# Gated attention and MoE layer: W2 loaded in four parts, its sums on VectorE, one product beside each up group

## The chip, the cores and the metric

The kernel runs on one core of a Trainium2 chip. The metric is the device time of one execution in microseconds (us); the table below gives the median of seven runs of the kernel before. The engines are called TensorE (PE in the profile; PEld is its weight load), VectorE (DVE), ScalarE (ACT), GpSimd (POOL) and SyncE (SP). Each engine works through its own instructions in the order in which the program puts them; an instruction that waits holds up everything behind it on the same engine.

## The reference

For each of 8 batches with 3008 rows, attention without softmax is multiplied by a gate and sent through a two-layer network:

```
scores = (1/S) * z @ z.T                  # z: 3008 x 64
out    = relu(scores)**2 @ v              # v: 3008 x 256
x      = u * out                          # 3008 x 256
h      = x @ w_in                         # w_in: 256 x 2048
g      = h * sigmoid(1.702 * h)
result = g @ w_out                        # w_out: 2048 x 256
```

The inputs and the result are float32. The kernel works in float16 with float32 accumulation.

## The kernel before, in words

**Tiles.** Rows of a batch are cut into 24 row tiles of 128 (the last one half full) and into 6 chunks of up to 512 (`NJ`, `NCH`). `W1` (w_in) and `W2` (w_out) stay in the on-chip memory as float16. `W2` has 16 slices of 128 rows (`NFF`), and 256 columns.

**Order by hand.** The order of instructions on every engine is the order in which the Python code issues them. Nothing reorders them later; only the waits are added, from what reads and writes what. Each kind of tile has a fixed number of buffers; a new tile takes the buffer of the oldest one and waits until that is no longer read.

**One batch.** Three stages follow each other.

- *Attention.* `attend` (line 270) gives for each chunk a list of steps, each of one or two matmuls; the loop at line 604 walks through them. Between steps the tables `SCHED0` (batch 0) and `SCHED` (later batches) say when `take` issues scores for later chunks, `TURN0` and `LOAD0` when a part of u is transposed on VectorE (`turn_u`) and the next loaded (`load_u`). When a chunk is done, VectorE multiplies it by u (`gate`, line 314), which makes the tile `xt`. In chunks of 47 steps that use half the rows of the array, step 24 on TensorE waits for a signal that passes through POOL's queue after step 23 (`post`, line 82).
- *Up groups and products.* An up group (`up_group`, line 335) makes 2 of 16 slices of the hidden layer for one chunk: 4 matmuls into the bank `hg` (2 buffers), the gelu on ScalarE from `hg` to `gf` (2 buffers), and a scaling on VectorE from `gf` to `gt`. There are 8 groups per chunk (`NFG`), 48 per batch. The first `LAGY` of them, 19, are spread over the steps of the last attention chunk, chunk 5 (line 614); they are called head groups. The other 29 follow in the loop at line 637.
  The second layer of chunks 0 to 3 is done with seven products of half size in place of eight (P1 to P7, lines 401 to 444). They need sums of parts of `gt` (`left_sum`, two instructions each of S1 to S4, on VectorE, one behind each up group from group 8 on) and sums of parts of W2 (`weight_sums`, line 368, into `WT`, once per run). A product is 16 matmuls of 128 columns. P6, P7 and P4 add into the bank that P1 opened, P3 into that of P5, P2 has its own; ScalarE copies the bank of P1 after P1, P6 and P7 (tiles `uP1`, `uP6`, `uP7`), before the next one may add to it. VectorE puts copy and bank together at P2, P7 and P3. In the loop at line 637 one product follows each up group as long as more than two are left: beside groups 19 to 44. Groups 45 and 46 have none, P4 of chunk 3 stands behind group 47, and P3 of chunk 3 behind that.
- *The last two chunks.* Their second layer (`down64`, line 487) is done directly and interleaved with the first scores of the next batch.

**Loading W2.** After attention chunk 4 of batch 0 POOL copies one element of its `xt` (so that it waits for the chunk), issues one 1 MB load of W2 that converts to float16, waits for it, and makes the four sums. Behind these in POOL's queue stand the loads of u and z of batch 1, the copies of z, and the conversion of v.

Of the kernel before, what the change touches and what calls it, by code (L numbers as in the profile page):

```python
# [10 lines left out]
F16 = mybir.dt.float16  # L11
P = 128
# [3 lines left out]
def kernel(  # L16
# [14 lines left out]
    ALU = mybir.AluOpType  # L31
# [5 lines left out]
    NJ = (S + P - 1) // P  # L37
# [39 lines left out]
    ZT, V16, UQ, UT, XT, unit, TT = {}, {}, {}, {}, {}, {}, {}  # L77
# [47 lines left out]
    def first_zt(g):  # L125
        z2 = ZT["st"][g // CB][:, g % CB * CB:(g % CB + 1) * CB]
        zp = ps1.tile([P, CB, P], F16, name="zp", tag="ps1")
        for k in range(CB):
            pe.transpose(zp[:, k, :], z2[:, k, :, :], ident)
        zt = ZT[0][:, g * CB:(g + 1) * CB, :].rearrange("d n p -> d (n p)")  # L130
        nb = CB if g < NCH - 1 else CB - 1
        dst = zt[:, :nb * P].rearrange("d (p n) -> d n p", n=nb)
        if g == 0:
            act.activation(dst, zp[:, :nb, :], AF.Copy, scale=1.0)
        else:
            dve.tensor_copy(dst, zp[:, :nb, :])
        if nb < CB:
            dve.tensor_copy(zt[:, nb * P:], zp[:, nb, :])
# [49 lines left out]

    def turn_u(b, i):
        n = width(i)  # L190
        ut = pu.tile([P, NCC, CH // QW, QW], F32, name="ut", tag="ut")
        UT[b, i] = ut
        dve.transpose(ut[:, :, :n // QW, :].rearrange("p k q t -> p q k t"), UQ.pop((b, i))[:, :n // QW])  # L193
# [171 lines left out]
    LO, HI = slice(0, NFF // 2), slice(NFF // 2, NFF)  # L365
    C0, C1 = slice(0, P), slice(P, D)

    def weight_sums():
        b11, b12, b21, b22 = W2[:, LO, C0], W2[:, LO, C1], W2[:, HI, C0], W2[:, HI, C1]
        t1, t2, t3, t4n = (WT[:, m] for m in range(4))  # L370
        pool.tensor_tensor(t1, b12, b11, ALU.subtract)
        pool.tensor_tensor(t2, b22, t1, ALU.subtract)
        pool.tensor_tensor(t3, b22, b12, ALU.subtract)
        pool.tensor_tensor(t4n, b21, t2, ALU.subtract)

    def left(b, k, h, odd):
        g = GT[b, k, h].rearrange("p f (m o t) -> p f m o t", o=2, t=P)
# [23 lines left out]
    def products():  # L401

        lst = []
        for k in range(NST):
            one = [(k, "P5"), (k, "P6"), (k, "P2"), (k, "P7")]
            lst += [(k, "P1")] + ([(k - 1, "P4"), (k - 1, "P3")] if k else []) + one
        return lst + [(NST - 1, "P4"), (NST - 1, "P3")]

# [110 lines left out]

        return turns, [lambda n=n: step(n) for n in range(len(order))]  # L520

    LAGY = 2 * NFG + 3
    HEAD = 2

    def pieces(b, i):
# [29 lines left out]
    TURN0 = {(i, (38, 28)[i] if i < 2 else NJ + 4 if i < NCH - 1 else 12): i for i in range(NCH)}  # L555
    LOAD0 = {(i, n): i + 2 for i, n in TURN0 if i + 2 < NCH}
    TURN = {(1, NJ + 4): 2, (2, NJ + 4): 3, (4, NJ + 4): 4, (5, 8): 5}
    LOAD = {(3, NJ + 4): 4, (4, NJ + 5): 5}

    FIRST_ZT = {3: 3, 11: 4, 19: NCH - 1}  # L560
# [11 lines left out]
    def take(b, n):  # L572
        if n:
            group = [queue.pop(0) for _ in range(n)]
            scores(b, group)
# [23 lines left out]
    for b in range(B):  # L599
        nup = NCH * NFG  # L600
        sched, turn, load = (SCHED, TURN, LOAD) if b else (SCHED0, TURN0, LOAD0)
        head = 0
        for i in range(NCH):
            for n, step in enumerate(attend(b, i, b == 0 and i < 2)):
                if b == 0 and i == 0 and n == 5:
                    load_u(0, 0)
                if b == 0 and i == 0 and n in FIRST_ZT:
                    first_zt(FIRST_ZT[n])
                if (i, n) in turn:
                    turn_u(b, turn[i, n])  # L610
                if (i, n) in load:
                    load_u(b, load[i, n])
                take(b, sched[i].get(n, 0))
                if i == NCH - 1 and n >= HEAD and (n - HEAD) * LAGY // (2 * NJ - 2 - HEAD) >= head and head < LAGY:
                    up_group(b, head)
                    head += 1
                step()
            if b == 0 and i in (0, 1, NCH - 2):
                hold = const.tile([P, 1], F16, name=f"hold{i}")
                pool.tensor_copy(hold, XT[b, i][:, 0, :1])  # L620
                if i < 2:
                    w1v = moe_w_in.rearrange("(q k c) f -> q c k f", k=NCC, c=QW)
                    for k in range(2 * i, 2 * i + 2):
                        pool.dma_start(W1[k * QW:(k + 1) * QW], w1v[k])
                elif i == NCH - 2:
                    pool.dma_start(W2, moe_w_out.rearrange("(fo p) c -> p fo c", p=P))
                    weight_sums()
        more = b + 1 < B
        if more:
            for i in range(2):  # L630
                load_u(b + 1, i)
            load_z(b + 1)
            for n0 in range(0, NJ, VB):
                load_v(b + 1, n0, sp)
            fill(b + 1)
        downs, prods = down_list(b), products()
        for q in range(head, nup):
            if more and q in (head + 14, head + 20):
                k = int(q == head + 20)
                turn_u(b + 1, k)  # L640
                load_u(b + 1, k + 2)
            up_group(b, q)
            if len(prods) > 2 or q == nup - 1:
                product(b, *prods.pop(0))
        while prods:
            product(b, *prods.pop(0))
        if more:
            while downs[0][0] < NCH - 2:
                down(b, *downs.pop(0))
            for k in range(NCH - 2, NCH):  # L650
                turns, steps = down64(b, k)
                at = {n: 3 - len(turns) for n in turns} | TAIL[len(turns)]
                for n, step in enumerate(steps):
                    take(b + 1, at.get(n, 0))
                    step()
        else:
            for d in downs:
                down(b, *d)
# [30 lines left out]
```

## Time and profile before

| what | value |
|---|---|
| median of seven runs | 1228.67 us (1219.86 to 1232.71) |
| the profiled execution's own time | 1219.86 us |
| its span, first to last instruction | 1217.8 us |
| mean granted clock of TensorE | 0.995 of full speed |
| busy: PE, DVE, ACT, POOL | 1198.5, 825.3, 768.3, 300.5 us |
| W2 load (line 626): start, issue, landing | 81.92, 1.16, 9.0 us after its start |
| four sums of W2 on POOL (lines 371 to 374) | 2.12, 2.45, 2.57, 2.57 us |
| `s` sums of 128x1024 on VectorE (lines 395, 397, 399), mean | 0.84, 0.74, 0.75 us |

The span is that of one execution seen by the hardware profiler; the device time lies about 2 us above it. Durations of matmuls overlap, since the next one starts while the last one drains: four matmuls of 512 columns show 1.03 us, but the next work starts 0.86 us after them. So stages are compared by start times. An idle time in brackets at the end of a timeline row is that of the engine just before the row, with what ended it.

### The profile page before, as it was taken

Reading aid. Unit: us, or ns where it says so; the run is one execution under the profiler, and the core shown is the slowest. Engines: PE = TensorE matmul, PEld = TensorE weight load, DVE = VectorE, ACT = ScalarE, POOL = GpSimd, SP = SyncE. Lnnn points to the kernel's source line nnn. Section 1 sums busy time; section 2 is a strip of 40 time slices with the busy share of each in tenths; the row PEclk is TensorE's granted clock in tenths of the full one; section 3 lists DMA queues with packets and bytes.
Section 4 is the critical chain, followed back from the end, with each engine's and each line's share of the span. In section 5 each row is a group of like instructions: output and inputs, shape, how many; then the busy total and the mean of one; then the engine's idle time right before and its main releaser. Section 6 shows DMA issues by size and latency. Waiting matters only on the chain.

```text
span 1217.8 us, 28022 instructions
## 1 busy us (share of the span) xinstructions
PE 1198.5 (98%) x11691; PEld 713.9 (59%) x11691; DVE 825.3 (68%) x1253; ACT 768.3 (63%) x897; POOL 300.5 (25%) x350
## 2 busy tenths in 40 slices
PE   8999999999999999999999999999999999999998
PEld 3344775567644676446765467544775447755576
DVE  7669956498554985459754597637966479554882
ACT  6776675476854768457683576836667376772763
POOL 5217500353004510045200451005500134001000
PEclk8999999999999999999999999999999999999999
DMA  9953579563794629956299553974449754596012
GB/s 225 170 79 62 171 160 172 97 127 107 145 166 97 143 84 172 149 91 148 88 167 159 85 136 93 188 137 76 143 108 185 133 88 147 114 173 112 1 36 70
DMA packets 370767, 152.31 MB, mean 125 GB/s; under 512 B 313200, under 2 KB 364272, under 8 KB 370640
## 3 DMA queue, kind: packets, MB, share of 16 engines
q1 hardware_dynamic: 328960, 113.16, 48.7%
q0 software_dynamic: 33552, 29.37, 12.8%
q10 hardware_dynamic: 8128, 8.00, 2.2%
q8 instruction: 91, 1.49, 0.5%
q14 instruction: 36, 0.29, 0.1%
HBM read 60.29 MB, written 24.64 MB: 70 GB/s over the span
## 4 chain that ended last, share of the span: by engine, by line
PE 92%; ACT 3%; DMA 2%; DVE 2%; issue 1%; ACTq 0%; SPq 0%
PE o L301 37%; PE hg L342 26%; PE st L424 16%; PE yp L503 6%; PE sc L216 5%; DMA tt<-a 2%; ACT rl L228 1%; PE yp L458 1%; ACT gf L350 1%; DVE gt L351 1%; ACT y L516 1%; DMA zf<-in_z_dram 0%; DVE a L242 0%; DVE zst L123 0%; ACTq L476 0%
## 5 line engine op out<-in xcount | busy, mean ns | idle before, releaser
L350 ACT ACTIVATE gf<-hg 128x1024 f32<-128x1024 f32 (+1 forms) x384 | 386.0, 1007 | 200.4 <-PE hg L342 163.2
L228 ACT ACTIVATE rl<-sc 128x1024 f16<-128x1024 f32 x311 | 307.0, 1024 | 216.1 <-PE sc L216 203.7
L301 PEld LDWEIGHTS <-V 64*128 64x128 f16 (+1 forms) x4052 | 231.9, 94 | 255.1 <-issue 10.5
L342 PE MATMUL hg<-xt,W 128*128 128x512 f16 (+1 forms) x1408 | 354.8, 375 | 4.0 <-ACT gf L350 4.0
L351 DVE TENSOR_SCALAR gt<-gf 128x1024 f16<-128x1024 f32 (+1 forms) x384 | 280.3, 730 | 90.6 <-ACT gf L350 86.2
L301 PE MATMUL o<-a,V 64*128 64x512 f16 (+2 forms) x2010 | 316.5, 373 | 0.4 <-DVE a L242 0.4
L242 DVE TENSOR_TENSOR a<-rl 128x1024 f16<-128x1024 f16 x276 | 192.1, 698 | 181.8 <-ACT rl L228 180.7
L186 POOL DMA_DIRECT2D uq<-in_u_dram x188 | 132.5, 712 | 604.8 <-PE sc L216 444.4
L301 PE MATMUL o<-tt,V 64*128 64x512 f16 (+1 forms) x1762 | 215.1, 376 | 3.8 <-DMA tt<-a 3.8
L342 PEld LDWEIGHTS <-W 128*128 128x128 f16 x1536 | 141.6, 98 | 126.5 <-issue 9.5
L424 PEld LDWEIGHTS <-gt 128*128 128x128 f16 x2048 | 125.1, 98 | 28.9
L216 PE MATMUL sc<-ZT 64*128 64x512 f16 (+1 forms) x692 | 121.7, 367 | 2.6 <-ACT rl L228 1.9
L171 POOL CAST V<-vst 128x512 f16<-128x512 f32 x96 | 90.2, 979 | 61.3 <-DMA vst<-in_v_dram 48.6
L424 PEld LDWEIGHTS <-s 128*128 128x128 f16 x1536 | 93.5, 98 | 19.5
L503 PE MATMUL yp<-W,gt 64*128 64x256 f16 x1664 | 103.9, 269 | 0.0
L503 PEld LDWEIGHTS <-gt 64*128 64x128 f16 x1664 | 80.4, 94 | 19.2 <-POOLq L84 4.0
L318 DVE TENSOR_TENSOR xt<-o,ut 128x512 f16<-128x512 f32 x80 | 51.5, 685 | 38.1 <-PE o L301 38.1
L424 PE MATMUL st<-WT,s 128*128 128x128 f16 x1024 | 67.6, 219 | 0.0
L424 PE MATMUL st<-W,gt 128*128 128x128 f16 x1024 | 67.6, 219 | 0.0
L424 PE MATMUL st<-WT,gt 128*128 128x128 f16 x1024 | 67.6, 219 | 0.0
L216 PEld LDWEIGHTS <-ZT 64*128 64x128 f16 x692 | 38.0, 94 | 41.6 <-issue 9.9
L193 DVE STREAM_TRANSPOSE ut<-uq 128x1024 f32<-128x1024 f32 (+1 forms) x48 | 58.3, 1215 | 0.0
(48 smaller groups left out, 611.2 us busy)
## 6 DMA issues: line engine op xcount, KB each, us to landing
vst<-in_v_dram SPq DMA_DIRECT2D x39, 512.0 KB, 5.0
uq<-in_u_dram POOLq DMA_DIRECT2D x156, 128.0 KB, 3.4
out_dram<-y SPq DMA_DIRECT2D x32, 512.0 KB, 3.7
out_dram<-y ACTq DMA_DIRECT2D x8, 512.0 KB, 4.3
tt<-a SPq DMA_TRANSPOSE x230, 3.6
uq<-in_u_dram POOLq DMA_DIRECT2D x32, 112.0 KB, 3.0
vst<-in_v_dram SPq DMA_DIRECT2D x8, 384.0 KB, 4.6
out_dram<-y ACTq DMA_DIRECT2D x7, 384.0 KB, 5.0
```

The source lines that it names most:

```text
L171: pool.tensor_copy(V16[b][:, n0:n0 + VB, k, :].rearrange("p n (q c) -> p n q c", c=QW), vst.rearrange("p n (q k c) -> p n q k c", k=NCC, c ...
L186: eng.dma_start(uq[k * QW:(k + 1) * QW, :n // QW].rearrange("t q k c -> t q (k c)"), src[:, :, cs])
L193: dve.transpose(ut[:, :, :n // QW, :].rearrange("p k q t -> p q k t"), UQ.pop((b, i))[:, :n // QW])
L216: pe.matmul(sc[:, r, :m * P], zt[h, 2 * kp + r, :], zt[h, (qi + 1) * CB - m:(qi + 1) * CB, :], start=True, stop=True,)
L228: act.activation(rl, sc, AF.Relu, scale=csc)
L242: dve.tensor_tensor(a, rl, rl, ALU.mult)
L301: ins = pe.matmul(acc[c][:, :n], V16[b][h, j, c, :], weights(b, i, j)[h], start=(k, m) == first[c], stop=(k, m) == final[c],)
L342: pe.matmul(hg[:, e, :n], W1[:, c, ff * P:(ff + 1) * P], XT[b, i][:, c, :n], start=(c == 0), stop=(c == NCC - 1),)
L350: act.activation(gf[:, :, :n], hg[:, :, :n], AF.Gelu_apprx_sigmoid, scale=1.0 / FSC)
L351: dve.tensor_scalar(g, gf[:, :, :n], FSC, None, ALU.mult)
L424: pe.matmul(bank[:, m, :], lhs()[:, f, m, :], right[:, ff, :], start=name in ("P1", "P2", "P5") and m == 0 and ff == 0, stop=ff == NFF // ...
L503: ins = pe.matmul(yp[s // per][:, s % per, :], GT[b, k, ff // CB][h, ff % CB, s * P:(s + 1) * P], W2[h, ff, :], start=new, stop=n == last[ ...
```

## The change

- W2 is loaded in four parts of four slices (256 KB each), at steps 4, 10, 27 and 33 of attention chunk 4 of batch 0. Before each, POOL copies one element of the `xt` of chunk 3. Parts 0 and 1 hold the upper half of W2, 2 and 3 the lower.
- The four sums of W2 are issued on VectorE, behind the first, third, fifth and seventh up group of chunk 5 of batch 0.
- `LAGY` is 20 rather than 19: 20 head groups in chunk 5, 28 groups in the loop behind it, in every batch.
- One product is issued behind each of these 28 groups, none after them.
- Within a block the order is P1, (P4 and P3 of the block before), P6, P5, P7, P2. It was P1, (P4, P3), P5, P6, P2, P7.

```diff
+    def load_w2(k):
+        hold = const.tile([P, 1], F16, name=f"hold2{k}")
+        pool.tensor_copy(hold, XT[0, NCH - 3][:, 0, :1])
+        fs = slice(k * CB, (k + 1) * CB)
+        pool.dma_start(W2[:, fs], moe_w_out.rearrange("(fo p) c -> p fo c", p=P)[:, fs])
+
     def weight_sums():
...
-        pool.tensor_tensor(t1, b12, b11, ALU.subtract)
-        pool.tensor_tensor(t2, b22, t1, ALU.subtract)
-        pool.tensor_tensor(t3, b22, b12, ALU.subtract)
-        pool.tensor_tensor(t4n, b21, t2, ALU.subtract)
+        return [
+            lambda: dve.tensor_tensor(t1, b12, b11, ALU.subtract),
+            lambda: dve.tensor_tensor(t2, b22, t1, ALU.subtract),
+            lambda: dve.tensor_tensor(t3, b22, b12, ALU.subtract),
+            lambda: dve.tensor_tensor(t4n, b21, t2, ALU.subtract),
+        ]
...
-            one = [(k, "P5"), (k, "P6"), (k, "P2"), (k, "P7")]
+            one = [(k, "P6"), (k, "P5"), (k, "P7"), (k, "P2")]
...
-    LAGY = 2 * NFG + 3
+    LAGY = 2 * NFG + 4
...
+    LOADW = {4: 0, 10: 1, NJ + 3: 2, NJ + 9: 3}
...
+                if b == 0 and i == NCH - 2 and n in LOADW:
+                    load_w2(LOADW[n])
...
                     up_group(b, head)
                     head += 1
+                    if b == 0 and head in (1, 3, 5, 7):
+                        weight_sums()[head // 2]()
...
-                elif i == NCH - 2:
-                    pool.dma_start(W2, moe_w_out.rearrange("(fo p) c -> p fo c", p=P))
-                    weight_sums()
...
             up_group(b, q)
-            if len(prods) > 2 or q == nup - 1:
-                product(b, *prods.pop(0))
-        while prods:
             product(b, *prods.pop(0))
```

More of the change, by code (lines that the diff above doesn't have):

```diff
@@ L616 @@
                     head += 1
+                    if b == 0 and head in (1, 3, 5, 7):
+                        weight_sums()[head // 2]()
                 step()
-            if b == 0 and i in (0, 1, NCH - 2):
+            if b == 0 and i < 2:
                 hold = const.tile([P, 1], F16, name=f"hold{i}")
                 pool.tensor_copy(hold, XT[b, i][:, 0, :1])
[L621 to L624, printed above, removed]
-                elif i == NCH - 2:
-                    pool.dma_start(W2, moe_w_out.rearrange("(fo p) c -> p fo c", p=P))
-                    weight_sums()
+                w1v = moe_w_in.rearrange("(q k c) f -> q c k f", k=NCC, c=QW)
+                for k in range(2 * i, 2 * i + 2):
+                    pool.dma_start(W1[k * QW:(k + 1) * QW], w1v[k])
         more = b + 1 < B
```

## The prediction

> **What bounds the kernel now.** First the page's busy shares and its wait list. TensorE is busy for 98% of the span, and all its waits for a compute engine or a DMA come to 14 us, so only two things can shorten the kernel: less matmul work (the change has the same 11,691 matmuls), or fewer of those holes. VectorE and ScalarE have a third of the span free as a mean, which says nothing of single stages.
>
> ```profile
> PE 1198.5 (98%) x11691; PEld 713.9 (59%) x11691; DVE 825.3 (68%) x1253; ACT 768.3 (63%) x897; POOL 300.5 (25%) x350
> ...
> PE hg L342 <- ACT gf L350: 5.0, 13, 1.1
> PE o L301 <- DMA tt<-a: 3.8, 3, 2.6
> PE sc L216 <- ACT rl L228: 1.9, 2, 1.0
> ```
>
> The largest entry, 5.0 us in 13 waits of an up group's matmuls for the gelu on ScalarE, is the one the change touches. TensorE's timeline puts five of the 13 (3.0 us) in chunk 5 of batch 0, and one of 0.25 us at the end of each of the 8 batches. So next the timelines of POOL, DVE and PE around 91 to 106 us (start, duration, instruction, idle time before it):
>
> ```profile
> 91.02 2.12 POOL L371 TENSOR_TENSOR WT<-W 128x1024 f16<-128x1024 f16 x1 [7.93 <-DMA W<-in_moe_w_out_dram]
> 93.22 2.44 POOL L372 TENSOR_TENSOR WT<-W,WT 128x1024 f16<-128x1024 f16 x1
> 95.63 2.57 POOL L373 TENSOR_TENSOR WT<-W 128x1024 f16<-128x1024 f16 x1
> 98.16 2.57 POOL L374 TENSOR_TENSOR WT<-W,WT 128x1024 f16<-128x1024 f16 x1
> ...
> 89.92 0.69 DVE L351 TENSOR_SCALAR gt<-gf 128x1024 f16<-128x1024 f32 x1 [0.38 <-ACT gf L350]
> 91.16 7.58 DVE L351 TENSOR_SCALAR gt<-gf 128x1024 f16<-128x1024 f32 x3 [0.55 <-ACT gf L350]
> 98.67 2.61 DVE L395 TENSOR_TENSOR s<-gt 128x1024 f16<-128x1024 f16 x1
> 101.19 0.68 DVE L351 TENSOR_SCALAR gt<-gf 128x1024 f16<-128x1024 f32 x1
> ...
> 94.86 1.02 PE L342 MATMUL hg<-xt,W 128*128 128x512 f16 x4 [0.31 <-ACT gf L350]
> 97.39 1.02 PE L342 MATMUL hg<-xt,W 128*128 128x512 f16 x4 [1.13 <-ACT gf L350]
> 99.91 1.84 PE L342 MATMUL hg<-xt,W 128*128 128x512 f16 x4 [1.13 <-ACT gf L350]
> ...
> 91.00:106.10 15.10, 12.12 (x50) 4.90 (x49) 14.94 (x14) 7.30 (x8) 15.00 (x10) 0.89 0.13 40
> ```
>
> While POOL makes the four sums, each gt instruction of VectorE takes 2.5 us in place of 0.69, exactly the length of one POOL sum; ScalarE then has no free gf buffer, and TensorE no free hg bank. The last row is the stage table (busy us by engine, then granted clock 0.89): inside it, from 100 to 103.4 us, the clock was granted at half, which doubles the matmuls there (1.84 us for four in place of 1.03).
>
> **The change, part by part.**
>
> 1. *The sums leave POOL.* What that stretch costs is read from starts, since matmul durations overlap. In batch 0 chunk 5 runs from its first up group at 81.21 us to the first product at 112.29: 31.08 us. In batch 1 the same work, with no hole, runs from 232.90 to 258.68: 25.78 us. The difference is 5.3 us: 3.0 of shown idle time, half of 3.4 us at half clock (1.7), and about 0.6 of pipeline refills. It is all on TensorE's path. All of it goes if nothing else stalls there: -5.3 us.
>
> Here two pages stand behind the rows. The Trainium skill's "SBUF — State Buffer" (SBUF: two separate sides) says that VectorE and GpSimd share a port pair that one holds for a whole instruction while the other blocks. The rows agree for these sums, but not in general: at 254.77 a POOL copy took 5.97 us beside VectorE instructions that stayed at 0.68, so the later one can also give way. "TensorE: Matmul & The Clock Gate" (Part 1: The HAM clock gate) says that an idle window of about 3.4 us halves the clock. Here 3 us of scattered idle time was followed by the half clock, 3.4 us long. By the page's rule these holes are too short, and the clock's 1.7 us would stay for some other reason: a gain of 3.6. I go by the row, 5.3, because no other stretch after the start has the half clock.
>
> 2. *The sums on VectorE.* Four more instructions of 128x1024 f16. The nearest row is s<-gt: 0.68 us, 0.60 from start to start: 2.4 us in all. They stand behind the 1st, 3rd, 5th and 7th up group, where VectorE idles 0.4 to 0.7 us before each gt. The tight place is the third sum: the transpose of u (1.1 us) follows it at once, so gt, sum and transpose take 0.6 + 0.6 + 1.1 = 2.3 us in a group of 1.28, and the next gt is 1.0 us late. How much is free: in the trace the gt at 91.16 (the first of three in 7.58 us) ended 1.8 us late and TensorE was 0.47 late (94.86, where the pace gives 94.39), so about 1.4 us is absorbed. 1.0 fits. Bounds: 0 and 0.6 us; I take 0.2.
>
> 3. *W2 in four parts, in chunk 4.* POOL's queue gets four copies of 0.2 us and four issues. The W1 parts of the same 256 KB took 0.55 us each to issue and 6.9 to 11.2 to land; the single W2 load 1.16 and 9.0. POOL is free at 69.86 (the u load ends). Parts 0 and 1 are issued by 71.4. Next in that queue is the signal (line 84) that step 24 of chunk 4 on TensorE waits for; step 23 ends near 74.7, so 3.3 us are spare. A rule speaks against it: in the same section of "SBUF — State Buffer" the Trainium skill says that VectorE can keep GpSimd from writing descriptors, a 620 ns transfer becoming 3100. With 3.1 per issue the two parts would end near 76.5, and TensorE would stand 1.8 us. In this trace 188 u issues from POOL took 0.63 to 1.2 us, many beside busy VectorE; I take the row: nothing. Parts 2 and 3 follow the signal: issued by 76.3, landed by 83 to 87.5. The first sum needs parts 0 and 1 (landed by 82.6) near 84.1, the second needs the rest near 86.7. A wait of up to 0.8 us there is below the 1.4 absorbed: nothing. Behind W2, POOL's loads for batch 1 start some 20 us earlier; the second half of u still waits for VectorE's transpose in chunk 5. SP's transposes and V loads follow the z copies, and the V casts, which stretch VectorE's instructions to 1.09, fall a few products after chunk 5, as they do in batch 1 (from 266.9) without a TensorE wait.
>
> 4. *One product beside each up group.* Before, up groups 45, 46 and 47 stand without a product between them, and gelu is slower than an up group. TensorE and ScalarE at the end of batch 1:
>
> ```profile
> 303.49 1.89 PE L342 MATMUL hg<-xo,W 128*128 128x512 f16 x8
> 305.63 1.02 PE L342 MATMUL hg<-xo,W 128*128 128x512 f16 x4 [0.25 <-ACT gf L350]
> ...
> 304.55 1.94 ACT L350 ACTIVATE gf<-hg 128x1024 f32<-128x1024 f32 x2 [0.46 <-PE hg L342]
> ```
>
> Two groups of 0.864 us from 303.49 end at 305.22; the third starts at 305.63, 0.41 us late. In even batches (384 columns, 0.65 us a group) it is 157.33 and 157.75: 0.42. With a product of 0.89 us after every group ScalarE has 1.5 to 1.75 us per gelu of 0.8 to 1.0. Eight batches: -3.3 us. The products and up groups themselves only move.
>
> 5. *A 20th head group.* It moves 0.864 us of matmul from the next stage into chunk 5, and the groups there stand 1.28 us apart on TensorE (0.864 and 2.2 attention steps of 0.189) in place of 1.30. VectorE needs 1.20 for gt and sum, and two xt gates of 0.6. In batch 1 it worked without a pause from 248.6 to 262.4 and was 0.3 us behind gelu near the end. The tighter pace adds 0.02 per group over 12 groups: 0.55 behind, still within 1.4. I take nothing; bound 0.3 us a batch, 2.4.
>
> 6. *P6 straight after P1.* In block 0 only one up group now lies between P1 and P6, which adds into the same bank and waits for ScalarE's copy uP1. Rows: gelu at 112.49, uP at 113.41 for 0.38, so done at 113.79; the product after the next up group starts at 114.05. 0.26 us to spare, with semaphores to be paid out of it. Later blocks have P4 and P3 between. Bounds: 0 and 0.5 us a batch; I take 0.07, 0.6 in all. P7 and P2 in the new order have two groups or more of cover, and P4's copy now precedes the next stage by one group more.
>
> *Sum*: -5.3 - 3.3 + 0.2 + 0.6 = -7.8 us on the profiled execution's 1219.86 (span 1217.8 and 2 us around it): 1212.1. That execution was the fastest of the seven; the median is 8.8 us above, for reasons no row shows, so I take the same 7.8 off it: **1220.9**, 0.63% less.
>
> **The rivals.**
>
> *The small waits give half of it back.* Parts 5 and 6 at their upper bounds: 2.4 + 4.0 in place of 0.6, so 1220.9 + 5.8 = 1226.7, no measurable change. For it: VectorE without pause in chunk 5, and 0.26 us of slack. Against: no TensorE wait there in seven batches.
>
> *The stall only changes its cause.* If the last W2 parts land late, the second sum waits at the head of VectorE's queue, gt behind it, gelu behind that, TensorE last. Landing at 92 rather than 87.5 would cost about 92 - 86.7 - 1.4 = 3.9 us and perhaps the clock's 1.7 again: the 5.3 is gone, 1226.5. Against: transposes, which slowed W1, are over by chunk 4 (DMA share 0.12 from 67 to 81 us).
>
> *More than the trace shows.* The slow half of the seven runs may hold a longer stall here: some 5 us more, 1216. Nothing speaks for it but the spread.
>
> *Slower.* P6 waits for uP1 in every batch, and each wait sends the clock to half for 3.4 us (1.7 lost): with a 0.6 us wait, 8 x 2.3 = 18 us, 1239. It decides from 1.75 us a batch (14 us). Against: the 0.25 us holes at each batch's end were never followed by a half clock.
>
> **How the numbers follow.** A measurement of this kernel can tell about 0.5%, 6.1 us, so faster means below 1222.5. The forecast has 0.60 with an own range of 1217 to 1224, five sixths of it below the limit; the half given back 0.19; the stall with another cause 0.06; more gain 0.09; slower 0.06. Faster 0.50 + 0.09 = 0.59; same 0.10 + 0.25 = 0.35; slower 0.06. The range takes in the gain of 1216 with its own spread and both cases near 1226.5: 1213 to 1229.
>
> **What would show it.** Right: gt at 0.7 us through chunk 5 of batch 0, the chunk near 26.6 us from first up group to first product, no half clock after the start, POOL without sums, no wait of hg before group 47, the wait of hg for gelu down from 5.0 to below 1 us. Wrong: a gt or WT instruction waiting for the W2 DMA, a wait of st for uP in each batch, a wait at step 24 of chunk 4, or a half clock at some other place.

## The result, and the profile after

| | before | after |
|---|---|---|
| device time, median | 1225.96 us (64 executions, 1215.24 to 1244.56) | 1214.41 us (27 executions, 1207.67 to 1236.13) |
| ratio, 95% interval | | 0.9915, 0.9897 to 0.9933 |
| profiled execution, its span | 1219.86 us, 1217.8 us | 1210.50 us, 1208.5 us |
| mean granted clock | 0.995 | 0.996 |

The kernel became faster by 0.85%, some 10 us; 7.8 us (0.63%) were forecast. The ratio leaves out slow executions, those more than 1.5% above the fastest of their kernel, so it is not the quotient of the two medians (0.9906, 11.6 us). A second series of the changed kernel, 22 executions beside other executions of the one before, gave 1219.26 us and 0.9941 (0.9919 to 0.9963), some 7 us. So the size is known to a few microseconds only, and the experiments below are largely about the reason for that.

First the busy shares of the kernel after, from its profile (busy time, share of the span, instructions):

```profile
PE 1194.9 (99%) x11691; PEld 723.2 (60%) x11691; DVE 822.7 (68%) x1257; ACT 769.7 (64%) x897; POOL 314.9 (26%) x352
```

Then its list of TensorE's waits (who waits, for whom: total us, times, longest):

```profile
PE o L301 <- DMA tt<-a: 2.5, 2, 2.1
PE sc L216 <- ACT rl L228: 1.9, 2, 1.0
...
PE hg L342 <- ACT gf L350: 0.5, 1, 0.5
```

The up groups' wait for gelu has gone from 13 times and 5.0 us to once and 0.5. VectorE has four instructions more, the sums of W2. The wait for transposed tiles fell from 3.8 to 2.5 us, which no part of the forecast had. Now the timelines of POOL and VectorE where the moved work stands:

```profile
70.32 0.77 POOL L372 DMA_DIRECT2D W<-in_moe_w_out_dram  x1
71.40 0.75 POOL L372 DMA_DIRECT2D W<-in_moe_w_out_dram  x1
...
75.43 0.74 POOL L372 DMA_DIRECT2D W<-in_moe_w_out_dram  x1 [0.26 <-issue]
76.79 0.74 POOL L372 DMA_DIRECT2D W<-in_moe_w_out_dram  x1
...
83.97 0.68 DVE L378 TENSOR_TENSOR WT<-W 128x1024 f16<-128x1024 f16 x1
84.72 0.69 DVE L351 TENSOR_SCALAR gt<-gf 128x1024 f16<-128x1024 f32 x1
86.03 0.69 DVE L351 TENSOR_SCALAR gt<-gf 128x1024 f16<-128x1024 f32 x1 [0.62 <-ACT gf L350]
86.64 0.69 DVE L379 TENSOR_TENSOR WT<-W,WT 128x1024 f16<-128x1024 f16 x1
...
89.05 0.69 DVE L380 TENSOR_TENSOR WT<-W 128x1024 f16<-128x1024 f16 x1
89.65 1.10 DVE L193 STREAM_TRANSPOSE ut<-uq 128x896 f32<-128x896 f32 x1
90.68 1.25 DVE L351 TENSOR_SCALAR gt<-gf 128x1024 f16<-128x1024 f32 x2
91.85 0.69 DVE L381 TENSOR_TENSOR WT<-W,WT 128x1024 f16<-128x1024 f16 x1
```

The parts of W2 landed 4.6 us (median) after their issue and no sum waits for one. The sums take 0.69 us, and gt beside them too, 2.5 before. The tight place (third sum, transpose of u, two gt) passes without an idle TensorE. Next, the stretches that set the end, on TensorE: first and last up group of chunk 5 of batch 0 with the first product, the one hole between them, and the products of batch 1, first and last, with the first `down64` matmul behind them:

```profile
81.16 1.03 PE L342 MATMUL hg<-xt,W 128*128 128x512 f16 x4
...
102.48 1.02 PE L342 MATMUL hg<-xt,W 128*128 128x512 f16 x4 [0.53 <-ACT gf L350]
...
107.63 1.03 PE L342 MATMUL hg<-xt,W 128*128 128x512 f16 x4
108.49 1.06 PE L432 MATMUL st<-W,gt 128*128 128x128 f16 x16
...
254.44 1.06 PE L432 MATMUL st<-W,gt 128*128 128x128 f16 x16
...
299.25 1.03 PE L342 MATMUL hg<-xo,W 128*128 128x512 f16 x4
300.11 1.06 PE L432 MATMUL st<-WT,gt 128*128 128x128 f16 x16
301.00 1.03 PE L342 MATMUL hg<-xo,W 128*128 128x512 f16 x4
301.87 1.06 PE L432 MATMUL st<-W,s 128*128 128x128 f16 x16
302.86 0.50 PE L511 MATMUL yp<-W,gt 64*128 64x256 f16 x6
```

The starts that they are compared with, in the kernel before: chunk 5 and first product of batch 0, the same of batch 1, and the first `down64` matmul of batch 1.

```profile
81.21 1.03 PE L342 MATMUL hg<-xt,W 128*128 128x512 f16 x4
...
112.29 1.06 PE L424 MATMUL st<-W,gt 128*128 128x128 f16 x16
...
232.90 1.03 PE L342 MATMUL hg<-xt,W 128*128 128x512 f16 x4
...
258.68 1.06 PE L424 MATMUL st<-W,gt 128*128 128x128 f16 x16
...
308.37 0.50 PE L503 MATMUL yp<-W,gt 64*128 64x256 f16 x6
```

Chunk 5 of batch 0 is 108.49 - 81.16 = 27.33 us from first up group to first product; before it was 31.08 with one group of 0.864 less. So 31.08 + 0.86 - 27.33 = 4.6 us went there. The later batches need 26.64 (25.78 before), so 0.69 us of stall is left. The up groups of the batch end follow a product without idle time: from first product to first `down64` matmul a batch takes 46.71 or 48.42 us where it took 47.98 or 49.69. That is 1.27 less, of which 0.86 is the group that moved to chunk 5, so 0.41 per batch and 3.3 us in all. The spans differ by 9.4: 4.6 + 3.3, and 1.4 in attention and down of batches 1 to 7 (515.5 us before, 514.1 after). There the waits for transposed tiles that the list shows fell from 1.2 to 0.5 us. But this stretch isn't steady: two more profiles of the kernel before, without any edit, have 517.1 and 516.4 us, and one more of the changed kernel 515.1.

The stretch that the forecast showed at a mean clock of 0.89 now reads as follows (length, then busy PE, PEld, DVE, ACT, POOL, granted clock, DMA share, GB/s):

```profile
91.00:106.10 15.10, 14.57 (x72) 6.83 (x70) 14.85 (x24) 11.35 (x12) 8.00 (x10) 1.00 0.69 88
```

TensorE is busy for 14.57 of 15.10 us at full clock, against 12.12 at 0.89. The DMA share rose from 0.13 to 0.69: batch 1's loads, no longer queued behind the sums on POOL, have moved into chunk 5.

### The profile page after: what moved, and what is told of

It reads as the page before. It is cut to its first block, busy times and chain, and to the rows that moved or that the text cites. A ratio compares the mean times of both kernels' runs of the same rounds, so it can differ in the third digit from the quotient of the medians.

```text
span 1208.5 us, 28037 instructions
## 1 busy us (share of the span) xinstructions
PE 1194.9 (99%) x11691; PEld 723.2 (60%) x11691; DVE 822.7 (68%) x1257; ACT 769.7 (64%) x897; POOL 314.9 (26%) x352
## 4 chain that ended last, share of the span: by engine, by line
PE 93%; DMA 2%; ACT 2%; issue 1%; DVE 1%; ACTq 0%; SPq 0%
PE o L301 37%; PE hg L342 27%; PE st L432 17%; PE yp L511 6%; PE sc L216 5%; DMA tt<-a 2%; ACT rl L228 1%; PE yp L466 1%; ACT y L524 1%; DVE a L242 0%; DMA zf<-in_z_dram 0%; DVE zst L123 0%; ACTq L484 0%; DVE ZT L136 0%; ACT gf L350 0%
## 5 line engine op out<-in xcount | busy, mean ns | idle before, releaser
L301 PEld LDWEIGHTS <-V 64*128 64x128 f16 (+1 forms) x4052 | 240.6, 94 | 244.7 <-issue 9.6
L351 DVE TENSOR_SCALAR gt<-gf 128x1024 f16<-128x1024 f32 (+1 forms) x384 | 276.8, 721 | 91.8 <-ACT gf L350 88.8
L186 POOL DMA_DIRECT2D uq<-in_u_dram x188 | 130.0, 698 | 603.7 <-PE sc L216 438.2
L151 POOL COPY zst<-zst 128x768 f16<-128x768 f16 x14 | 58.3, 4161 | 50.2 <-DMA zst<-in_z_dram 50.2
```

The source lines that it names most:

```text
L151: pool.tensor_copy(zst[:, :, 1, :], zst[:, :, 0, :])
L301: ins = pe.matmul(acc[c][:, :n], V16[b][h, j, c, :], weights(b, i, j)[h], start=(k, m) == first[c], stop=(k, m) == final[c],)
L351: dve.tensor_scalar(g, gf[:, :, :n], FSC, None, ALU.mult)
```

## The experiments

Three kernels came first: each half of the change alone, and the early load with the sums still on POOL.

**The weights' half alone**: the kernel before with W2 in four early loads and the sums on VectorE, the old groups and products.

```diff
-        pool.tensor_tensor(t1, b12, b11, ALU.subtract)
...
+            lambda: dve.tensor_tensor(t1, b12, b11, ALU.subtract),
...
+                if b == 0 and i == NCH - 2 and n in LOADW:
+                    load_w2(LOADW[n])
```

> Only the weight half of the change: W2 in four parts in chunk 4 and its sums on VectorE; 19 head groups, the old order of products and their old places. My theory (the two halves add): chunk 5 of batch 0, from first up group to first product, falls from 31.1 us to 25.8 to 26.6, no half clock after the start, the eight holes of 0.41 us at the batch ends stay; the ratio to the kernel before is 1 - 5/1226 = 0.996. Rival (the surplus over the forecast comes from this half, since some executions of the kernel before stall longer there than the profiled one): ratio 0.994 or lower. Rival (the products' half carries it): 0.999 to 1.001.

Measured: 1216.62 us, 0.9943 (0.9916 to 0.997). Chunk 5 of batch 0 is 25.95 us, 0.17 above the other batches, with no half clock; the products still take 47.98 and 49.69 us, so the holes at the batch ends stay.

**The products' half alone**: the kernel before with `LAGY` 20, one product per group and the new order.

```diff
-    LAGY = 2 * NFG + 3
+    LAGY = 2 * NFG + 4
...
-            if len(prods) > 2 or q == nup - 1:
-                product(b, *prods.pop(0))
-        while prods:
             product(b, *prods.pop(0))
```

> Only the other half: 20 head groups, one product beside each of the 28 later groups, the new order within a block; the W2 load and its sums on POOL as before. My theory: the eight holes at the batch ends go (8 x 0.41 = 3.3 us), the stall in chunk 5 of batch 0 stays at about 5.3 us with its half clock; ratio 1 - 3.3/1226 = 0.9973. Rival (the surplus is in this half, something in the later batches that the page of one execution did not show): 0.995 or lower. Rival (P6 close behind P1 gives the gain back): 0.999 or higher.

Measured: 1223.03 us, 0.9977 (0.995 to 1.0004). The products take 46.71 and 48.42 us in the later batches, 0.41 less per batch net, as in the full change. Chunk 5 of batch 0 is 33.44, 6.8 us over 26.64, for here the half clock came at the end of the stall and reached past it (120.4 to 123.8 us, while the last POOL sum ended at 118.2). This profile has a wait of 17.4 us for a transposed tile in batch 0; a second profile of the same half, on the quiet base below, has the same 6.8 us (33.48), with half clock from 97.8 to 104.6 and the last sum done at 98.8. TensorE in the first (start, duration, idle time before):

```profile
117.36 1.02 PE L342 MATMUL hg<-xt,W 128*128 128x512 f16 x4 [1.13 <-ACT gf L350]
118.23 0.54 PE L301 MATMUL o<-a,V 128*128 128x448 f16 x2
120.50 1.87 PE L342 MATMUL hg<-xt,W 128*128 128x512 f16 x4 [1.73 <-ACT gf L350]
122.16 0.95 PE L301 MATMUL o<-a,V 128*128 128x448 f16 x2
122.91 1.47 PE L342 MATMUL hg<-xt,W 128*128 128x512 f16 x4
```

The halves add: 0.9943 x 0.9977 = 0.992, the whole 0.9915 and 0.9941.

**Early load, sums on POOL**, with the old groups and products: is it the place of the load or the engine of the sums?

```diff
-            lambda: dve.tensor_tensor(t1, b12, b11, ALU.subtract),
+            lambda: pool.tensor_tensor(t1, b12, b11, ALU.subtract),
...
+            if b == 0 and i == NCH - 2:
+                for sum_ in weight_sums():
+                    sum_()
```

> The kernel before with W2 loaded in four parts in chunk 4, as in the change, but the four sums still on POOL, behind chunk 4: they start when W2 has landed, near 83 to 86 us rather than 91. My theory (it matters on which engine the sums are, since POOL's sums keep VectorE from its gt): each gt beside a sum still takes 2.1 to 2.6 us, chunk 5 keeps 3 to 5.3 of its 5.3 us of stall, ratio 0.999 to 1.001. Rival (the early load is what helps: the sums would then be done while VectorE has no s sums to make, and its spare time takes them): chunk 5 near 27 us and ratio 0.996.

Measured: 1223.12 us, 0.999 (0.9965 to 1.0015). Chunk 5 is only 1.4 us too long (27.17), but a new wait of 1.8 stands before it. POOL, VectorE, TensorE:

```profile
81.00 2.14 POOL L378 TENSOR_TENSOR WT<-W 128x1024 f16<-128x1024 f16 x1
...
80.48 3.21 DVE L242 TENSOR_TENSOR a<-rl 128x1024 f16<-128x1024 f16 x1 [0.22 <-ACT rl L228]
...
86.08 0.66 PE L301 MATMUL o<-a,V 64*128 64x448 f16 x3 [1.78 <-DVE a L242]
```

While a POOL sum ran, VectorE's attention instruction took 3.21 us in place of 0.69. So sums on POOL cost 3.2 us earlier too (1.4 + 1.8): the engine is a cause of its own. The rest of the 5.3, some 2 us, is left for the late load; it follows from these two numbers alone, for the ratio's interval reaches from a loss of 2 us to a gain of 4.

**The kernel before, two more profiles** (no edit), to see how long its stall is.

> The kernel before, unchanged, profiled a second time on the same chip as the others. If the stall in chunk 5 of batch 0 is a matter of order alone, it is 5.3 us again within 0.5 (31.1 us from first up group to first product) with one half clock of 3.4 us; if it varies from execution to execution and so explains a gain above the forecast, it is 7 us or more, or has a second half clock. The holes at the batch ends should be 0.41 us each again.

> The kernel before, a third profile. Its stall in chunk 5 of batch 0 was 5.3 us (with a half clock inside it) and 5.8 us (without one), and 6.8 us in the kernel with the products' half alone. If it is VectorE that sets it, and the half clock adds only where it reaches past the sums, it is again between 5.2 and 7.

Measured: 1224.46 and 1223.61 us, with chunk 5 of batch 0 at 31.59 and 30.96 us: stalls of 5.8 and 5.2, and in neither a half clock in that stretch. A fourth profile, on the quiet base below, has 31.05 us and no half clock either. TensorE in the first:

```profile
99.65 1.02 PE L342 MATMUL hg<-xt,W 128*128 128x512 f16 x4 [1.12 <-ACT gf L350]
...
102.18 1.02 PE L342 MATMUL hg<-xt,W 128*128 128x512 f16 x4 [1.13 <-ACT gf L350]
...
105.31 1.02 PE L342 MATMUL hg<-xt,W 128*128 128x512 f16 x4 [1.54 <-ACT gf L350]
```

Four matmuls take 1.02 us here, 1.84 in the profile of before, yet the stall is no shorter. So VectorE's pace beside the sums sets it, and a half clock inside it fills time in which TensorE would have waited.

**The old order of the products** in the changed kernel.

```diff
-            one = [(k, "P6"), (k, "P5"), (k, "P7"), (k, "P2")]
+            one = [(k, "P5"), (k, "P6"), (k, "P2"), (k, "P7")]
```

> The changed kernel with the old order within a block (P5, P6, P2, P7); everything else as changed. My theory: with one up group between any two products neither order makes TensorE wait, so the stage from first product to the last two chunks stays at 46.7 us in even batches and 48.4 in odd ones, as in the changed kernel, and the order is worth nothing. Rival: P6 directly behind P1 pays for the copy uP1; then the old order would be 0.1 to 0.5 us a batch shorter.

Measured: chunk 5 of batch 0 27.33 us, products 46.71 and 48.42, the changed kernel's numbers to 0.01. The order is worth nothing in these stages. The one execution took 1227.91 us because of a 16.5 us wait for a transposed tile in batch 0, which the order does not touch.

**W2 late**: the changed kernel with one load of W2 behind chunk 4.

```diff
-                if b == 0 and i == NCH - 2 and n in LOADW:
-                    load_w2(LOADW[n])
...
+                pool.dma_start(W2, moe_w_out.rearrange("(fo p) c -> p fo c", p=P))
```

> The changed kernel with W2 loaded in one piece after chunk 4, as before (landing near 91 us), so that the first sum on VectorE has to wait for it from about 84 us. If VectorE can be 1.4 us late before TensorE feels it, as I took from one gt, TensorE stands 7.0 - 1.4 = 5.6 us in chunk 5, which becomes about 32.2 us long in place of 26.6. If what can be absorbed is larger (two gf and two hg buffers are some two up groups, 2.6 us), about 31 us. If nothing is absorbed, 33.6. This is the rival of the forecast in which the stall only changes its cause, made on purpose.

Measured: chunk 5 36.05 us, 9.4 over 26.64, more than any number expected. VectorE, TensorE and the stretch's row:

```profile
97.52 0.69 DVE L378 TENSOR_TENSOR WT<-W 128x1024 f16<-128x1024 f16 x1 [7.38 <-DMA W<-in_moe_w_out_dram]
98.13 1.29 DVE L351 TENSOR_SCALAR gt<-gf 128x1024 f16<-128x1024 f32 x2
...
99.99 1.87 PE L342 MATMUL hg<-xt,W 128*128 128x512 f16 x4 [6.32 <-ACT gf L350]
...
100.00:106.00 6.00, 6.00 (x15) 2.22 (x15) 3.78 (x7) 2.90 (x3) 2.20 (x4) 0.50 0.13 33
```

The wait passed from gt over gelu to TensorE, nearly whole. Then TensorE ran for 6.0 us at half clock, unbroken, which cost another 3.0: 6.3 + 3.0 = 9.3, against 9.4 measured. This is the rival "the stall only changes its cause"; in the changed kernel itself it does not occur, since W2 lands in time.

**z of batch 1 held until chunk 5 is over**, in the changed kernel. The one hole left (102.48) stands behind these rows of POOL and VectorE, in which a copy of z has come into chunk 5:

```profile
98.67 1.10 POOL L151 COPY zst<-zst 128x768 f16<-128x768 f16 x1 [3.10 <-DMA zst<-in_z_dram]
...
99.01 1.31 DVE L405 TENSOR_TENSOR s<-s,gt 128x1024 f16<-128x1024 f16 x1
100.24 1.07 DVE L351 TENSOR_SCALAR gt<-gf 128x1024 f16<-128x1024 f32 x1
```

```diff
+            if b == 0:
+                hold = const.tile([P, 1], F16, name="holdz")
+                pool.tensor_copy(hold, XT[b, NCH - 1][:, 1, :1])
```

> The changed kernel with the z loads of batch 1, and POOL's copy of them, held back until chunk 5 of batch 0 is done. The hole of 0.52 us before an up group in chunk 5 comes, in my reading, from that copy (1.1 us on POOL, in which an s sum on VectorE takes 1.31 us in place of 0.68) on top of VectorE's four W2 sums. Then the hole goes and chunk 5 of batch 0 is 26.65 us, as in the later batches. If the W2 sums alone make VectorE too late, the hole stays and chunk 5 is 27.3 us.

Measured: chunk 5 26.64 us, no hole. So what was held back, z's loads and copy, is its cause, and the rows above point to the copy; the four sums alone cost nothing. With 19 head groups the same copy, beside the four sums, made no hole (the weights' half: 0.17 us in all, and 0.26 in a second profile below); with 20 it costs 0.7 to 1.0 us. So it seems to need the tighter pace of the 20th group too. The execution's 1214.78 us contain a wait of 5.8 us for a transposed tile in batch 0.

**Is W1 what makes batch 0 wait?** Up to here TensorE had waited 0 to 17.4 us for transposed tiles in batch 0 of one execution, while W1 was loaded between the transposes (landing 8.5 to 15.6 us after issue, the median of each profile). Three kernels load the second half of W1 (twice) or all of it behind step 25 of chunk 3, in the changed kernel; beside the first the changed kernel ran again.

```diff
+                if b == 0 and i == NCH - 3 and n == NJ + 1:
+                    load_w1(0)
+                    load_w1(1)
...
-            if b == 0 and i < 2:
...
-                    pool.dma_start(W1[k * QW:(k + 1) * QW], w1v[k])
```

> The changed kernel with the second half of the W1 load moved from the end of chunk 1 (43 us) to step 25 of chunk 3 (about 63 us), where the transposes are over. The profiles so far differ by 0 to 17 us in waits of TensorE for a transposed tile in batch 0 between 45 and 65 us, while the DMA queues are full. If the W1 load is what makes them late, these waits go: first up group at 78 to 79.5 us, and a ratio to the kernel before of 0.988 or lower, below that of the changed kernel in the same call. If the queues are full without it, or W1 now lands too late for the first up group at 81 us, the ratio is that of the changed kernel or worse.

> The changed kernel again, beside the others of this call. My theory (the stall of chunk 5 in the kernel before is 5.3 to 6.8 us in the profiles so far, 3.3 us at the batch ends, 0.7 us given back): ratio 0.9925 within 0.002. If the first measurement held something more lasting than that: 0.9915 or lower. Its profile should have chunk 5 of batch 0 at 27.3 us within 0.2, with one hole of some 0.5 us.

> The same kernel as the one with half of the W1 load moved, a second time. Its first ratio to the kernel before was 0.9919 with an interval of 0.0025 on each side, and the changed kernel beside it had 0.9941. If moving the load helps, it is 0.990 to 0.993 again; if the first was chance, 0.9925 to 0.995 as for the changed kernel.

> The changed kernel with the whole W1 load at step 25 of chunk 3 (about 63 us), none of it while the transposes of chunks 0 to 2 run. If the W1 loads are what crowds the DMA queues before that, the long waits for a transposed tile (16 to 17 us in two profiles) become rarer still than with one half moved: ratio 0.988 or lower, highest time below 1225. If the 2 MB then land only after the first up group is due at 80 us, TensorE waits at the head of chunk 5 for them, 2 to 8 us, and the ratio is 0.993 or higher.

Measured: half of W1 later, 1213.15 us (0.9919, 0.9894 to 0.9944) and 1215.55 (0.9939, 0.9907 to 0.997), not to be told from the changed kernel; the changed kernel itself 1219.26 (0.9941). All of W1 later: **1206.62 us, 1205.65 to 1209.56, 0.9855 (0.9822 to 0.9888)**, faster than both kernels. A second series of it (below) gave 1207.34 and 0.9857. In its profile no matmul waits for a transposed tile (one weight load does, 0.4 us), and W1 lands sooner (KB each, median us to landing):

```profile
W<-in_moe_w_in_dram POOLq DMA_DIRECT2D x4, 256.0 KB, 4.8
```

**Both kernels and both halves on the quiet base.** With all of W1 loaded at step 25 of chunk 3, which is called the quiet base here, executions of a kernel lie within a few microseconds, so the parts can be weighed.

> The kernel before with nothing changed but the W1 load, which stands at step 25 of chunk 3. With the changed kernel so altered the times lay within 4 us (1205.7 to 1209.6), so the effect of the change can be measured on this quiet base. If the stages tell all (5.2 to 5.8 us of stall in chunk 5, 3.3 at the batch ends, 0.7 given back: 8.0 net), this kernel takes 1214.6 us, within 1. If the change does more than the stages of the profiles show (10.4, as first measured), 1217 or above. If the forecast of 7.8 was right, it can not be told from the first.

> The weights' half of the change alone, on the quiet base (W1 load at step 25 of chunk 3). By the stages it is 3.3 us above the changed kernel on that base less the 0.5 us that chunk 5 gives back with 20 head groups: near 1209.5. If the weights' half does more than its stages, the difference to the kernel before on the quiet base is above 6 us; by the stages it is 5.1 to 5.6.

> The products' half alone on the quiet base. By the stages, 3.3 us below the kernel before on that base, if the stall in chunk 5 stays the same with 20 head groups: near 1211.3. If a half clock that reaches past the stall (6.8 us in one profile) is usual here, near 1212.5.

> The changed kernel with the whole W1 load at step 25 of chunk 3, a second time: 1206.6 us within 1, the reference for the three others; ratio to the kernel before 0.9855 within 0.003.

**What the weights' half gains beyond its stall.** Two kernels differ from the changed one on that base in one thing each: W2 in one load in place of four (at the same early step), and the sums on POOL behind chunk 4.

```diff
-    LOADW = {4: 0, 10: 1, NJ + 3: 2, NJ + 9: 3}
+    LOADW = {4: 0}
```

> The changed kernel on the quiet base (W1 loaded whole in chunk 3), with W2 in one load at step 4 of chunk 4 instead of four, its sums on VectorE as in the change. Open: why the weights' half gains about 2.5 us more than its two stages there, as shorter waits for transposed tiles in batches 1 to 7. If the single load is what slows the transposes' queue for the whole run (its share 47.5% instead of 44%, packets 28 ns instead of 25 to 26): attention and down of batches 1 to 7 sum to 515 to 517 us and the time is 1209 to 1210. If it is the engine of the sums: share 44%, sum 513, time 1206.6 to 1207.4 as with four loads.

> The changed kernel on the quiet base with W2 in four early loads, but its sums on POOL behind chunk 4. The sums' own stall is 3.3 us (1.8 before chunk 5 and 1.4 in it, from the run of the same edit on the other base). If four loads suffice for the faster transposes: share of their queue 44%, attention and down of batches 1 to 7 sum to 513 us, time 1207 + 3.3 = 1210 to 1210.5. If the sums on POOL are what slows them: share 47.5%, sum 515 to 517, time 1212 to 1214.

Measured on the quiet base (attention and down: sum of batches 1 to 7, from a batch's first `down64` matmul to the next batch's first up group; share: time that the packets of the queue q1 took, of 16 DMA engines' span; q1 carries the transposes, most loads of v and most results; each from one profile). The rows "one load" and "sums on POOL" come from another chip than the rest, where the kernel before on its old base took 1223.71 us beside 1224.97, so what they differ by from the others is uncertain by about a microsecond.

| kernel | time, range (us) | ratio to before, 95% | W2 loads, sums | attention and down | share |
|---|---|---|---|---|---|
| before | 1217.94, 1214.86 to 1220.25 | 0.9939, 0.9918 to 0.9959 | one, POOL | 517.2 | 47.6% |
| products' half | 1215.95, 1213.47 to 1216.76 | 0.9923, 0.9893 to 0.9953 | one, POOL | 515.1 | 47.6% |
| changed, one load | 1209.26, 1208.19 to 1211.49 | 0.9881, 0.9849 to 0.9913 | one, VectorE | 514.6 | 47.9% |
| weights' half | 1210.01, 1209.57 to 1210.40 | 0.9878, 0.9849 to 0.9907 | four, VectorE | 513.1 | 43.3% |
| changed, sums on POOL | 1210.19, 1209.24 to 1210.56 | 0.9885, 0.985 to 0.992 | four, POOL | 512.9 | 43.0% |
| changed | 1207.34, 1206.47 to 1208.40 | 0.9857, 0.9825 to 0.989 | four, VectorE | 512.8 | 44.2% |

The full change takes off 1217.94 - 1207.34 = 10.6 us here. The kernel before had been expected at 1214.6 from the stages, and the 3 us that it lies above this are what the last two kernels were to explain. The products' half is 2.0 of it on the old weights, where its chunk 5 stalls longer (33.48 us), and 2.7 on the new (3.2 in its own stage, less 0.7 that chunk 5 then takes more). The sums on POOL cost 1210.19 - 1207.34 = 2.9, or 3.6 against the other series of the changed kernel (1206.62); 3.3 was expected from their stall. One load in place of four costs 1.9 to 2.6 (the time expected if the single load slows the transposes; the sum of 514.6 us is just under the 515 expected), though no wait of TensorE goes back to W2. The queue q1 shows it for "one load" and for "sums on POOL" (packets, MB, share of 16 engines):

```profile
q1 hardware_dynamic: 328960, 113.16, 47.9%
```

```profile
q1 hardware_dynamic: 328960, 113.16, 43.0%
```

The same packets take 7 to 10% less time in the whole run wherever W2 came in four parts on this base, whichever engine sums, and there batches 1 to 7 hold no wait of a matmul for a transposed tile. Where W2 came in one part they hold 0.4 to 3.4 us of such waits. On the old base the changed kernel's share is 48.0%, with four loads.

So far it looks as if the split of the load gained 2 us. But the traces show that it is not the loads themselves that act: the queue is about as much faster before any part of W1 or W2 is issued. Here are the first 60 us of "products' half" (one load) and "weights' half" (four), from the same chip; W1 is issued from 61.2 us on and W2 later still:

```profile
q1 hardware_dynamic: 26912, 9.18, 82.3%
```

```profile
q1 hardware_dynamic: 26896, 9.18, 73.2%
```

That is 29.4 and 26.1 ns a packet (share x 16 engines x 60 us, over the packets). All three kernels with one load have 29.4 to 30.5 there, all four profiles with four loads 26.1 to 27.8. So the programs seem to differ in something that holds from the start, and one such thing is where their tiles lie. Each load of W2 that waits for a chunk makes a one-element tile `hold`, and so do the loads of W1 in their old place. In the built programs such a tile takes 32 bytes of each partition and shifts all tiles behind it. The faster kernels have exactly four, and their tiles start at multiples of 512 bytes; all others have one, three, five, six or seven, and their tiles start elsewhere. This fits all 20 profiles, but no run changes the placement alone. So the 2 us went with the four loads on this base; that the split of the load is their cause isn't shown, and the placement is a rival that nothing here tests. Nor is it settled why the kernel before waits 2 us longer for these tiles than the products' half does, each in one profile (that of the kernel before is of its slowest execution, 1220.25 us).

## Why the prediction was right or wrong

The direction and the mechanism held: in the two profiles the two stages gave 4.6 + 3.3 = 7.9 us, where the sum had 7.8. **The step that failed is what the forecast did with TensorE's wait for transposed tiles**, the second row of its own wait list (3.8 us). The sum has no term for it, and the level calls its effect "reasons no row shows". In the runs this wait is 0 to 17.4 us in batch 0 of an execution, and it sets both the level and most of the spread. 1214.41 lies in the range of 1213 to 1229, but 6.5 us below 1220.9 and below the likeliest case's own 1217 to 1224. Of the 6.5, 2.7 are the level; 3.8 are that the medians differ by 11.6 rather than 7.8 us. Part of these 3.8 is chance, since the second series of the changed kernel, 1219.26, is inside 1217 to 1224. Two things are luck. Part 1 was 0.7 too large and parts 2 and 6 together 0.8 too dear, so the errors cancel. And the range holds only because its lower end was set for a longer stall in chunk 5, which did not come.

- *The level.* "The median is 8.8 us above, for reasons no row shows, so I take the same 7.8 off it" failed twice. Seven executions gave 1228.67, 64 gave 1225.96: 2.7 us. And a row did show the reason: TensorE's wait for transposed tiles, 2.6 of its 3.8 us in batch 0. It lies between 0 and 17.4 us in the profiles with W1 in its old place, and the first up group of batch 0 starts there at 78.3 to 98.6 us. With all of W1 in chunk 3 no matmul waits for such a tile in batch 0 in any of the seven profiles, the first up group starts at 78.9 to 81.1 us, and ranges of 29 us (64 and 27 executions) shrink to 5.4 and 3.9 (ten executions each, the changed kernel's from its two series). Whoever compares two kernels of this family on the old base reads this wait along with the change.
- *Part 1, -5.3.* Without the z copy it is exactly 5.3 (31.08 + 0.86 - 26.64), with it 4.6. Its split into 3.0 idle, 1.7 half clock and 0.6 refills was wrong: two profiles of before without any half clock there stall for 5.2 and 5.8. A better working, argued and not tested, is four POOL sums, beside each of which one VectorE instruction takes 2.5 us in place of 0.69, some 7 us more in all, less what the buffers of gf and hg absorb. The Trainium skill's "TensorE: Matmul & The Clock Gate" (Part 1: The HAM clock gate), which wants an idle window of about 3.4 us, was set against the row and put aside. Scattered holes of 4.6 us in one stretch went without half clock in the first extra profile, as the page has it. In the profile of before, and in both profiles of the products' half, such holes were followed by it, though none was longer than 1.1 us in the one and 1.7 in the other. What decides isn't shown. The gain was nearly right since the half clock of that profile lay under the wait, not beside it.
- *Part 2, +0.2.* 0 (z held back) to 0.26 (weights' half, with the copy of z). The tolerance of 1.4 us was too large: of 7.46 us by which gt was late with W2 late, 6.48 reached TensorE, so 1.0 was absorbed. Beside the copy of z two VectorE instructions lost 0.6 and 0.4, and TensorE 0.69: there, where sums fill VectorE's pauses, only 0.3 was absorbed.
- *Part 3, nothing.* Right for the queue at step 24 and for the landing of W2; POOL's issues took 0.74 to 0.77 us. Wrong in what it moved forward: it named the V casts and the u load, but the copy of z came into chunk 5 and took 0.7 us back (1.0 on the quiet base). And the kernels with the split were about 2 us faster on the quiet base, for a reason that stays open.
- *Part 4, -3.3.* Right to 0.01 us per batch in the changed kernel; with one product per group batches 1 to 7 show it in every profile but one (0.06 in one batch), and batch 0 is up to 0.6 us longer in the products' half.
- *Parts 5 and 6, 0 and +0.6.* Part 6 costs nothing: the old order gives the same stages. Part 5 costs next to nothing in the later batches: chunk 5 is 25.78 + 0.86 = 26.64 there, but in five other profiles one or two batches show 26.84 to 26.92. In batch 0 it made the copy of z felt.

Of the rivals, small waits didn't come. W2 late happens only when it is made late. A wait of P6 for uP1, the way to a slower kernel, does not appear in the changed kernel (the products' half alone had one wait of 0.4 us for such a copy). "More than the trace shows" had the nearest number, 1216, with the wrong place: the stall in chunk 5 was 5.2 to 5.8 us in four profiles of the kernel before, and not the longer the slower the execution. The rest of the gain lies in attention and down, 1.4 us in the two profiles compared, half of it shown as waits for transposed tiles.

On the quiet base the two stages give 31.05 + 0.86 - 27.61 = 4.3 and 3.2 us, 7.5 of the 10.6 measured, again close to the forecast's 7.8. The other 3 us are not in what the forecast summed: about 2 went with the four loads and the faster queue, and the rest is within what single profiles and series of four to ten executions can tell.

## What to carry to other kernels

Here two-input sums on POOL stretched the VectorE instructions beside them to the sums' own length (2.5 us in place of 0.69). So put such sums on VectorE where it has pauses that take them, and then look at what else moves forward in POOL's queue. Give every up group that waits for ScalarE some matmul work beside it, and count stages from start to start, which here gave the gain per batch to 0.01 us. Before a change of half a per cent is weighed, find the wait that spreads the executions and remove it: moving all of one weight load out of the transposes' stretch was worth 7 us (1224.97 to 1217.94 for the kernel before), and made the rest measurable. And when two kernels differ over the whole run, compare them first in a stretch that lies before the edit: what differs there already isn't the edit's work, but may come from what it did to the program's layout.

## What the hardware showed that was not expected

- One idle stretch of 6.3 us on TensorE was followed by 6.0 us of work at half clock, 3.0 us more; holes of 0.4 to 1.5 us that add up to 4.6 were followed by no half clock in one execution, but holes of 0.7 to 1.7 (4.5 in all) by 3.4 us of it in another, and holes of 0.5 to 1.1 (3.3 in all) by 6.8 us in a third.
- With 1 MB of W1 loaded in four parts among the transposes of batch 0, TensorE waited anywhere from 0 to 17.4 us for transposed tiles there, in executions of nearly the same program, and the parts themselves landed after 8.5 to 15.6 us (medians); loaded later in the batch they took 4.8 to 5.5, and no matmul of batch 0 waited.
- The packets of queue q1 took 7 to 10% less time through the whole run in four profiles of three kernels (shares of 43.0 to 44.2%) than in all others (47.4 to 48.7%). On the quiet base the difference is there in the first 60 us, before any weight is loaded (26.1 to 27.8 ns a packet beside 29.4 to 30.5). Only in these three kernels do the tiles start at multiples of 512 bytes; whether that is the cause isn't tested.
